# A drain of GpSimd in mid-run and another order of the first loads, in a kernel of a DFT, a channel mix and routed experts

## The chip, the cores and the metric

One core of one Trainium2 chip runs one program. The metric is device time in microseconds (us), first to last instruction of the core with the little that lies around it. In the text PE is the matmul engine (TensorE), DVE is VectorE, ACT is ScalarE, POOL is GpSimd and SP is SyncE, which here only issues DMAs. A "q" behind a name (SPq, POOLq) marks what an engine's sequencer does: issue, wait, branch, drain.

## The reference

```
X = fft(fft(x, axis=1), axis=2).real                  # x: 4 x 3072 x 256
xk, xr = mixes of X and X shifted by one position (mu_k, mu_r)
r = sigmoid(xr @ w_r);  y = r * (relu(xk @ w_k)**2 @ w_v)      # 256 -> 1024 -> 256
e = argmax(y @ w_gate);  g = softmax prob of e * sigmoid(y @ w_output_gate)[e]
out[token] = g * (relu(y @ w1[e]) @ w2[e])            # 8 experts, 12288 tokens
```

Four weights arrive as 64-bit floats and are turned into pairs of 32-bit parts (high and low) on the chip.

## The kernel before

Tile (the framework) orders the instructions of each engine by their priority, which follows the order in which the program text creates them, and by what they wait for. Each engine then runs its list in order.

**The first stage (lines 262 to 384).** `load_first_x` (L262) issues the load of the DFT constants and seven loads of `x` for batch 0 on SP's queue, and after them four loads of weights (`convert_r`, then three `convert_k`, L259 and L157). `a_steps` (L274) makes the first DFT pass: 13 PE products (L288) from the seven `xs` tiles, each copied back from PSUM by ACT (L102), and each finished `xs` tile is written to a scratch tensor `scr` in DRAM (L298, L301): from POOL's queue for batch 0, from ACT's queue for batches 1 to 3. When all seven writes have landed, `load` (L307) reads `scr` back transposed, as `raw` tiles (L312). DVE adds and subtracts halves of `raw` (`s`, `t`, `f`), PE makes the second pass (`ps`, L364) with the tables `tb`, then the passes over the channels, and the result is `xt`. `mix_steps` (L396) makes the inputs `rh`, `rl`, `kh`, `kl` of the first of 24 blocks (`b_block`, L498).

**Weight conversion.** `convert` (L202) issues a load into a `both` tile and notes it; `convert_rest` (L220) converts the oldest one: ACT takes the absolute value (`g`, L225), DVE shifts and masks the halves (`a`, `b`, `w`, five operations), ACT rounds to the high part `h`, and DVE makes the low part with two subtractions and additions. There are nine such units, one of `w_r`, four of `w_k`, four of `w_v`. At the top level (L554 to L572) the text stands in this order: first loads, `setup_first`, `setup_second` (the constant `mc`), the 13 products, two conversions, the first group of the second pass, the fifth weight load, a third conversion, and so on.

**The middle.** 24 blocks (512 positions each) run on PE with DVE and ACT; POOL writes each block's token numbers into expert lists (`lists`, 96 indirect DMAs, L491).

**The last stage.** `make_plan` (L721) makes on DVE a table `plan` of which expert each tile of 256 tokens belongs to. `extra` (L893, through the helper of L890) loads one number of it into a register of each engine. `pipeline` (L809) then runs 25 full tiles and five half tiles (numbers 55 to 59): it gathers tokens (L621, 55 indirect DMAs by POOL), multiplies by the expert's weights and stores with POOL (`out<-o`, L707, 55 indirect DMAs, one for each half tile, of which the stores of 55 to 59 are the last five). Behind it stands a conditional block (L895, `tc.If(extra > 0)`) for token counts that don't fit, which is skipped with this data. At the end of the program (L926) each engine drains and all of them meet.

The lines that matter most:

```
267        for i, (pool, tag, bufs) in enumerate(places):
269            load_x(first_x[i], 0, i)
270        for unit in early_units[:4]:
271            unit()
298   (POOL if b == 0 else ACT).dma_start(sv[:, :, 2 * w - 2:2 * w + 2], e...)
707   i = POOL.indirect_dma_start(out[:, :], bass.IndirectOffsetOnAxis(ap=ix[:, u, 1:2], axis=0),
893   extra = value(NTILE, NTILE + E, ...)
894   pipeline(list(range(-EARLY, MORE[0])) + list(range(NTILE, NTILE + HALVES)), EARLY)
895   with tc.If(extra > 0):
```

Of the kernel before, what the change touches and what calls it, by code (L numbers as in the profile page):

```python
# [26 lines left out]
EARLY = 3  # L27
MORE = [22, 26, 31, 38, NTILE]
HALVES = 5
CAP = NT + TT  # L30
ROW = 265
FAR = 1 << 20
# [63 lines left out]
def moe_kernel(ctx: ExitStack, tc: tile.TileContext, x, mu_k, mu_r, wk2, wv2, wr2, wg, wo, w1, w2,  # L96
# [4 lines left out]
    def act_copy(o, i, scale=1.0):  # L101
        return ACT.activation(out=o, in_=i, func=ACTF.Copy, scale=scale)  # L102
# [49 lines left out]
    def follow(i, earlier, kind, reason):  # L152
        for k in earlier:
            tc.add_manual_dep(i.ins, k.ins.name, mybir.DependencyInfo(kind, mybir.DependencyReason.DATA), reason=reason)

    def load_later(o, i):
        follow(SP.dma_start(o, i), raws[1:2], mybir.DependencyClass.NoSync, "the first groups come first")  # L157

    def split(h, l, src, eng=None):
        return act_copy(h, src), tt(l, src, h.bitcast(F32), ALU.subtract, eng)  # L160
# [23 lines left out]
    def setup_second():  # L184
        mc = bp.tile([128, 2, 2, 128], F32, name="mc", tag="y", bufs=1)
        SP.dma_start(mc, c_m.rearrange("p (a b c) -> p a b c", a=2, b=2))
        split(mh, ml, mc)
# [29 lines left out]
        load_later(both.rearrange("p (a b) -> p a b", a=src.shape[1]), src.bitcast(I32))  # L217
        loaded_w.append((h, l, both, a, b, g))

    def convert_rest():  # L220
        h, l, both, a, b, g = loaded_w.pop(0)
        lo, hi = both[:, 0:1024:2], both[:, 1:1024:2]
        w = bp.tile([128, 512], F32, name="cw", tag="mx")
        af, bf = a.bitcast(F32), b.bitcast(F32)
        ACT.activation(out=g, in_=hi.bitcast(F32), func=ACTF.Abs)  # L225
        DVE.tensor_scalar(a, hi, 3, 0x3FFFFFF8, ALU.logical_shift_left, ALU.bitwise_and)
        stt(a, hi, -0x40000000, a, ALU.bitwise_and, ALU.bitwise_or)
        stt(af, g, SMALLEST, af, ALU.is_ge, ALU.mult)
        DVE.tensor_scalar(b, a, -0x800000, None, ALU.bitwise_and)
        stt(w, lo.bitcast(U32), 2.0 ** -52, bf, ALU.mult, ALU.mult)  # L230
        flat = lambda t: t.rearrange("p a b -> p (a b)")
        act_copy(flat(h), af)
        tt(af, af, flat(h).bitcast(F32), ALU.subtract)
        tt(flat(l), af, w, ALU.add)

# [27 lines left out]
    def load_first_x():  # L263
        places = [(a1, "xs", 3)] * 3 + [(bp, "yh", 1), (bp, "yl", 1), (bp, "rs", 1), (bp, "row", 2)]
        SP.dma_start(fc, c_f)
        for i, (pool, tag, bufs) in enumerate(places):
            first_x.append(pool.tile([120, 2, 512], F32, tag=tag, name="xs", bufs=bufs))
            load_x(first_x[i], 0, i)
        for unit in early_units[:4]:
            unit()  # L270

    def a_steps(b):
        scr = dram.tile([24, 130, 256], F32, name="scr", tag="scr", bufs=2)
        sv = scr.rearrange("s (g m) d -> s g m d", g=5)  # L274
        for w in range(13):
            if w % 2 == 0:
                if b == 0:
                    e = xs = first_x[w // 2]
                else:
                    xs = a1.tile([120, 2, 512], F32, tag="xs", name="xs", bufs=3)  # L280
                    i = load_x(xs, b, w // 2)
                    follow(i, raws[2:3], mybir.DependencyClass.NoSync, "the first groups come first")
                    e = a1.tile([120, 2, 512], F32, tag="e", name="e", bufs=2)
            k_ = 120 if w < 12 else 96
            fs = slice(0, 120) if w < 12 else slice(120, 216)
            ps = pm.tile([120, 512], F32, tag="m", name="ps1")
            if b == 0:
                PE.matmul(ps[0:k_], fc[0:k_, fs], xs[0:k_, w % 2], start=True, stop=True)  # L288
                yield
            else:  # L290
                h = a1.tile([120, 512], F32R, tag="xh", name="xh")
                l = a1.tile([120, 512], F32R, tag="xl", name="xl")
                split(h[0:k_], l[0:k_], xs[0:k_, w % 2])
                yield
                mm3(ps[0:k_], fh[0:k_, fs], fl[0:k_, fs], h[0:k_], l[0:k_])
            act_copy(e[0:k_, w % 2], ps[0:k_])
            if w % 2:
                (POOL if b == 0 else ACT).dma_start(sv[:, :, 2 * w - 2:2 * w + 2], e.rearrange("p w d -> p (w d)"))  # L298
                yield
            elif w == 12:  # L300
                (POOL if b == 0 else ACT).dma_start(sv[:, 0:4, 24:26], e[0:96, 0])  # L301
            yield
        loaded = {}

# [248 lines left out]

    load_first_x()  # L554
    setup_first()
    setup_second()
    advance(0, 32)
    convert_rest()
    convert_rest()
    advance(0, 1)  # L560
    early_units[4]()
    convert_rest()
    advance(0, 4)
    setup_third()
    convert_rest()
    advance(0, 5)
    for _ in mix_steps(BLOCKS[0]):
        pass
# [5 lines left out]

    c1 = {}
    weights, xtile, meta, index, chunks, regs = {}, {}, {}, {}, {}, {}
    hq, outs, stores = {}, {}, []

    def open_c1():
        sa.close()  # L580
# [17 lines left out]
    def width(t):  # L598
        return 2 if t < NTILE else 1
# [88 lines left out]
    def m2(t, p):  # L688
        if p == 0:
            outs[t] = [pm.tile([128, D], F32, tag="m", name=f"o{u}") for u in range(width(t))]  # L690
        h, l = hq.pop((t, p))
        for u in range(width(t)):
            for a in range(2):
                f = 2 * p + a
                wh, wl = weights[t][2 + f // 4]
                cols = slice((f % 4) * D, (f % 4) * D + D)
                tok = slice(u * 128, u * 128 + 128)
                ps = outs[t][u]
                PE.matmul(ps, h[:, a, tok], wh[:, cols], start=f == 0, stop=False)  # L699
                PE.matmul(ps, l[:, a, tok], wh[:, cols], start=False, stop=False)  # L700
                PE.matmul(ps, h[:, a, tok], wl[:, cols], start=False, stop=f == 7)  # L701
        if p == 3:
            sc, ix = meta.pop(t), index.pop(t)
            o = bp.tile([128, 2, D], F32, tag="t1", name="o", bufs=2)
            for u in range(width(t)):
                ACT.activation(out=o[:, u], in_=outs[t][u], func=ACTF.Copy, scale=sc[:, u])
                i = POOL.indirect_dma_start(out[:, :], bass.IndirectOffsetOnAxis(ap=ix[:, u, 1:2], axis=0),  # L707
                                            o[:, u], None, bounds_check=NT - 1, oob_is_err=False)
                for k in stores[-4:]:
                    tc.declare_no_dep(i.ins, k.ins, reason="every token is in one list once: rows are distinct")  # L710
                stores.append(i)
            outs.pop(t)
            weights.pop(t)

# [171 lines left out]
    for _ in tail:  # L886
        pass
    sb.close()
    make_plan()
    value = lambda i, top, why: nc.values_load(  # L890
        c1["plan"][0:1, i:i + 1, 3:4].rearrange("p a b -> p (a b)"), min_val=0, max_val=top,
        skip_runtime_bounds_check_because=why)
    extra = value(NTILE, NTILE + E, "what is left of sums that add up to at most NTILE and E")  # L893
    pipeline(list(range(-EARLY, MORE[0])) + list(range(NTILE, NTILE + HALVES)), EARLY)
    with tc.If(extra > 0):  # L895
        total = value(0, NTILE, "a sum of rounded counts that add up to at most NT")
        halves = value(NTILE + 1, E, "at most one half tile of each expert")
# [32 lines left out]
```

## Time and profile before

| what | value |
|---|---|
| median of 3 runs | 1190.78 us (1190.38 to 1191.68) |
| the profiled execution's own time | 1189.58 us |
| its span, first to last instruction | 1187.8 us |
| busy: PE, DVE, ACT, POOL | 96%, 75%, 65%, 19% of the span |
| mean granted PE clock | 0.985 of full speed |
| DMAs issued by POOL | 96 + 55 + 55 indirect, 7 plain |

Busy time is what the profiler records of an engine's instructions; a PE that is busy is not a PE at its peak. The chain is the sequence of work that ended last, followed back from the end. Idle time of an engine counts only where that engine stands in the chain.

### The profile page before, as it was taken

What the parts mean: (1) busy time and instruction counts of PE and PEld (TensorE: products, weight loads), DVE (VectorE), ACT (ScalarE), POOL (GpSimd) and SP (SyncE); (2) the same over time, 40 slices, a digit from 0 to 9 for tenths busy, and PEclk for the clock granted to TensorE, in tenths of its full rate; (3) what the DMA queues carried; (4) which work ended last, traced back from release to release, by engine and by line L of the source; (5) the groups of instructions that cost most, each with busy time, mean ns of one, the idle gap of its engine ahead of it and who ended that gap; (6) DMA issues with size and microseconds to landing.
All of it is one profiled execution on the core that took longest, in us unless ns stands there. A gap on an engine that the chain in (4) does not pass through costs nothing.

```text
span 1187.8 us, 19728 instructions
## 1 busy us (share of the span) xinstructions
PE 1135.6 (96%) x6743; PEld 971.6 (82%) x6743; DVE 892.6 (75%) x2032; ACT 775.3 (65%) x1611; POOL 228.4 (19%) x228
## 2 busy tenths in 40 slices
PE   5499999999999999999999999999999999999994
PEld 1477888888888888888887888877999999999994
DVE  1899898578869768768857877776677777777782
ACT  3577777567777667767756666855376676667671
POOL 1000111111100111111111111123342433343220
PEclk9699999999999999999999999999999999999998
DMA  8753551214432215324100000202234133441580
GB/s 275 235 183 126 157 160 55 88 57 130 128 126 81 81 54 144 76 65 128 48 28 29 28 28 19 90 20 55 88 119 147 47 113 109 118 124 38 156 246 13
DMA packets 63176, 119.17 MB, mean 100 GB/s; under 512 B 14299, under 2 KB 41181, under 8 KB 62297
## 3 DMA queue, kind: packets, MB, share of 16 engines
q1 hardware_dynamic: 51015, 91.62, 25.2%
q0 software_dynamic: 9296, 16.76, 4.6%
q10 hardware_dynamic: 2754, 9.44, 2.8%
q8 instruction: 55, 0.90, 0.4%
q14 instruction: 56, 0.46, 0.2%
HBM read 116.43 MB, written 46.57 MB: 137 GB/s over the span
## 4 chain that ended last, share of the span: by engine, by line
PE 87%; DMA 3%; DVE 3%; issue 3%; ACT 1%; SPq 1%; POOL 0%; POOLq 0%; ACTq 0%
PE v L252 8%; PE v L253 7%; PE v L254 7%; PE psk L252 7%; PE psk L253 7%; PE psk L254 7%; PE hps L254 4%; PE hps L253 4%; PE hps L252 4%; PE o L701 4%; PE o L700 4%; PE o L699 4%; PE ps L364 4%; PE ps L252 2%; PE psr L252 2%
## 5 line engine op out<-in xcount | busy, mean ns | idle before, releaser
L491 POOL DMA_INDIRECT lists<-cid,pi x96 | 100.9, 1051 | 683.9 <-DVE pi L488 622.3
L108 DVE SCALAR_TENSOR_TENSOR t<-psk,t 128x512 f32<-128x512 f32 x192 | 132.3, 689 | 62.5 <-ACT t L530 60.3
L530 ACT ACTIVATE t<-psk 128x512 f32<-128x512 f32 x192 | 114.3, 597 | 97.6 <-PE psk L254 84.8
L105 DVE TENSOR_TENSOR ql<-t,qh 128x512 fp32r<-128x512 f32 x192 | 132.4, 690 | 37.0 <-ACT qh L102 35.2
L252 PE MATMUL psk<-kh,wkh 128*128 128x512 f32 x384 | 156.6, 408 | 2.2 <-DVE t L108 1.2
L252 PE MATMUL v<-qh,wvh 128*128 128x512 f32 x384 | 153.7, 400 | 0.2 <-ACT qh L102 0.2
L253 PE MATMUL v<-qh,wvl 128*128 128x512 f32 x384 | 152.0, 396 | 0.0
L253 PE MATMUL psk<-kh,wkl 128*128 128x512 f32 x384 | 151.6, 395 | 0.0
L254 PE MATMUL psk<-kl,wkh 128*128 128x512 f32 x384 | 151.1, 394 | 0.0
L254 PE MATMUL v<-ql,wvh 128*128 128x512 f32 x384 | 150.2, 395 | 0.0
L102 ACT ACTIVATE qh<-t 128x512 fp32r<-128x512 f32 x192 | 120.7, 629 | 42.3 <-DVE t L108 35.4
L684 ACT ACTIVATE hh<-hps 128x512 fp32r<-128x512 f32 (+1 forms) x120 | 67.4, 562 | 107.6 <-PE hps L254 89.9
L108 DVE SCALAR_TENSOR_TENSOR hl<-hps,hh 128x512 fp32r<-128x512 f32 (+1 forms) x120 | 77.5, 646 | 73.7 <-ACT hh L684 63.1
L621 POOL DMA_INDIRECT xg<-rows,ix x55 | 61.5, 1119 | 183.0 <-PE hps L254 48.1
L252 PEld LDWEIGHTS psk<-kh,wkh 128*128 128x128 f32 x384 | 72.5, 189 | 17.6 <-DVE t L108 1.6
L254 PEld LDWEIGHTS v<-ql,wvh 128*128 128x128 f32 x384 | 72.3, 188 | 17.2 <-DVE ql L105 0.4
L254 PEld LDWEIGHTS psk<-kl,wkh 128*128 128x128 f32 x384 | 72.3, 188 | 16.7
L252 PEld LDWEIGHTS v<-qh,wvh 128*128 128x128 f32 x384 | 72.3, 188 | 15.3 <-ACT qh L102 0.9
L253 PEld LDWEIGHTS psk<-kh,wkl 128*128 128x128 f32 x384 | 72.6, 189 | 14.2
L253 PEld LDWEIGHTS v<-qh,wvl 128*128 128x128 f32 x384 | 72.5, 189 | 14.3
L108 DVE SCALAR_TENSOR_TENSOR mx<-xt,omu,mx 128x512 f32<-128x512 f32 x96 | 71.9, 749 | 6.3 <-ACT mx L402 5.3
L105 DVE TENSOR_TENSOR wlb<-raw,whb 128x512 fp32r<-128x512 f32 x112 | 73.3, 686 | 2.5 <-ACT whb L102 0.8
(219 smaller groups left out, 3102.5 us busy)
## 6 DMA issues: line engine op xcount, KB each, us to landing
raw<-in_moe_w SPq DMA_DIRECT2D x112, 512.0 KB
rows<-row SPq DMA_DIRECT2D x24, 530.0 KB
raw<-scr SPq DMA_DIRECT2D x24, 512.0 KB
out<-zeros SPq DMA_DIRECT2D x48, 256.0 KB
xs<-in_x SPq DMA_DIRECT2D x24, 480.0 KB
scr<-e ACTq DMA_DIRECT2D x18, 480.0 KB
tb<-in_c_t SPq DMA_DIRECT2D x20, 256.0 KB
scr<-xs POOLq DMA_DIRECT2D x6, 480.0 KB
```

The source lines that it names most:

```text
L102: return ACT.activation(out=o, in_=i, func=ACTF.Copy, scale=scale)
L105: return (eng or DVE).tensor_tensor(out=o, in0=a, in1=b, op=op)
L108: return DVE.scalar_tensor_tensor(out=o, in0=a, scalar=s, in1=b, op0=op0, op1=op1, **kw)
L252: PE.matmul(ps, ah, bh, start=start, stop=False)
L253: PE.matmul(ps, al, bh, start=False, stop=False)
L254: return PE.matmul(ps, ah, bl, start=False, stop=stop)
L364: PE.matmul(ps[:, a * 128:a * 128 + 128], f[:, a, c, par * 128:par * 128 + 128], tb[:, a, c], start=c == 0, stop=c == 1)
L491: i = POOL.indirect_dma_start(lists[:, :], bass.IndirectOffsetOnAxis(ap=pi[:, u:u + 1], axis=0), cid[:, n, u], None, bounds_check=E * CAP ...
L530: ACT.activation(out=t, in_=ps, func=ACTF.Relu)
L621: POOL.indirect_dma_start(xg[:, u], None, rows[0:nr], bass.IndirectOffsetOnAxis(ap=ix[:, u, 0:1], axis=0), bounds_check=nr - 1, oob_is_err ...
L684: marks[:] = [last, ACT.activation(out=h, in_=ps, func=ACTF.Relu), stt(l, ps, 0.0, h.bitcast(F32), ALU.max, ALU.subtract)]
L699: PE.matmul(ps, h[:, a, tok], wh[:, cols], start=f == 0, stop=False)
```

## The change

- **Drain.** After the store of half tile 57 (`DRAIN_AT = NTILE + HALVES - 3`), POOL gets a drain instruction. It is ordered behind that store and ahead of the stores of 58 and 59, on POOL alone.
- **Count.** The load of `extra` into registers is created after `pipeline` instead of before it.
- **Loads dealt.** The loads of `w_r` and of two parts of `w_k` are issued after the second, third and fourth load of `x`, not after the seventh; the fourth weight load comes after the 13 products in the text, as does `setup_second`.
- **Conversions.** The first three run on DVE alone (the absolute value as a mask, the rounding as a copy) and are created before the 13 products; the fourth is created after the first group.
- **Scratch writes.** Those of batch 0 are issued on ACT's queue, as those of the other batches are.

```diff
+DRAIN_AT = NTILE + HALVES - 3
...
-    def convert_rest():
+    def convert_rest(alone=False):
...
-        ACT.activation(out=g, in_=hi.bitcast(F32), func=ACTF.Abs)
+        if alone:
+            DVE.tensor_scalar(g.bitcast(I32), hi, 0x7FFFFFFF, None, ALU.bitwise_and)
+        else:
+            ACT.activation(out=g, in_=hi.bitcast(F32), func=ACTF.Abs)
...
-        act_copy(flat(h), af)
+        DVE.tensor_copy(flat(h), af) if alone else act_copy(flat(h), af)
...
             load_x(first_x[i], 0, i)
-        for unit in early_units[:4]:
-            unit()
+            if 1 <= i <= 3:
+                early_units[i - 1]()
...
-                (POOL if b == 0 else ACT).dma_start(sv[:, :, 2 * w - 2:2 * w + 2], e.rearrange("p w d -> p (w d)"))
+                ACT.dma_start(sv[:, :, 2 * w - 2:2 * w + 2], e.rearrange("p w d -> p (w d)"))
...
     setup_first()
+    for _ in range(3):
+        convert_rest(True)
+    advance(0, 32)
+    early_units[3]()
     setup_second()
-    advance(0, 32)
-    convert_rest()
-    convert_rest()
     advance(0, 1)
     early_units[4]()
+    advance(0, 4)
     convert_rest()
-    advance(0, 4)
     setup_third()
-    convert_rest()
     advance(0, 5)
...
                 stores.append(i)
+                if drains and t > DRAIN_AT:
+                    follow(i, drains[:1], mybir.DependencyClass.NoSync, "what is written from here on is retired at the end")
+            if t == DRAIN_AT:
+                drains.append(POOL.drain())
+                follow(drains[0], stores[-width(t):], mybir.DependencyClass.NoSync, "this much is retired first")
...
+    pipeline(list(range(-EARLY, MORE[0])) + list(range(NTILE, NTILE + HALVES)), EARLY)
     value = lambda i, top, why: nc.values_load(
...
     extra = value(NTILE, NTILE + E, "what is left of sums that add up to at most NTILE and E")
-    pipeline(list(range(-EARLY, MORE[0])) + list(range(NTILE, NTILE + HALVES)), EARLY)
     with tc.If(extra > 0):
```

## Rows read from the trace of the kernel before

**Rows 1.** Windows of the first stages: span, busy by engine, clock, DMA share, GB/s

```profile
25.90:46.40 20.50, 7.57 (x27) 5.97 (x28) 18.46 (x42) 9.79 (x28) 2.21 (x4) 0.50 0.72 237
46.40:60.00 13.60, 9.04 (x47) 7.48 (x47) 11.63 (x27) 9.94 (x26) 0.00 (x0) 0.88 0.84 257
60.00:80.00 20.00, 17.74 (x89) 14.05 (x88) 19.36 (x38) 14.02 (x32) 0.00 (x0) 1.00 0.61 194
120.00:140.00 20.00, 20.00 (x101) 16.05 (x100) 17.17 (x36) 15.22 (x36) 4.37 (x4) 1.00 0.42 123
```

**Rows 2.** Chain of what ended last, first 40 us: start, us, what

```profile
8.29 19.09 DMA both<-in_moe_w_k
...
30.37 4.86 DMA scr<-xs
35.38 3.86 DMA raw<-scr
39.26 0.69 DVE s L105
```

**Rows 3.** ACT in order of time: start, us, instruction, idle time before it

```profile
25.07 0.68 ACT L225 ACTIVATE cg<-both 128x512 f32<-128x512 f32 x1 [7.26 <-DMA both<-in_moe_w_r]
...
27.40 0.68 ACT L225 ACTIVATE cg<-both 128x512 f32<-128x512 f32 x1 [0.69 <-DMA both<-in_moe_w_k]
...
28.98 1.07 ACT L102 ACTIVATE xs<-ps 120x512 f32<-120x512 f32 x2
```

**Rows 4.** POOL's first write, and DMA queues with packets from 11.19 to 16.4 us

```profile
11.19 0.77 POOL L298 DMA_DIRECT2D scr<-xs  x1 [8.45 <-ACT xs L102]
...
q1 hardware_dynamic: 338, 1.26, 104.6%
```

**Rows 5.** DVE in order of time, before and after the first raw tile

```profile
25.07 0.43 DVE L226 TENSOR_SCALAR ca<-both 128x512 int32<-128x512 int32 x1 [21.53 <-DMA both<-in_moe_w_r]
...
42.20 0.68 DVE L105 TENSOR_TENSOR wkl<-ca,cw 128x512 fp32r<-128x512 f32 x1
...
48.38 0.69 DVE L105 TENSOR_TENSOR wkl<-ca,cw 128x512 fp32r<-128x512 f32 x1
```

**Rows 6.** Group of DVE's mask operations, first 100 us: busy, mean ns, idle

```profile
L226 DVE TENSOR_SCALAR ca<-both 128x512 int32<-128x512 int32 x5 | 2.1, 425 | 21.9 <-DMA both<-in_moe_w_r 21.5 <-DMA both<-in_moe_w_k 0.4
```

**Rows 7.** POOL's last three stores in order of time

```profile
1158.09 0.98 POOL L707 DMA_INDIRECT out<-o,ix  x1 [7.44 <-ACT o L706]
1166.48 0.98 POOL L707 DMA_INDIRECT out<-o,ix  x1 [7.42 <-ACT o L706]
1171.97 0.98 POOL L707 DMA_INDIRECT out<-o,ix  x1 [4.51 <-ACT o L706]
```

**Rows 8.** Sequencers at the end: ns min/median/max, first and last start in us

```profile
L890 SPq TENSOR_LOAD <-plan x1: 273/273/273, 1155.4 to 1155.4; - x1
...
L890 POOLq TENSOR_LOAD <-plan x1: 498/498/498, 1171.7 to 1171.7; - x1
...
L895 POOLq EVENT_SEMAPHORE  x5: 17/42/43, 1175.2 to 1175.7; - x5
...
L895 POOLq INC_SWDGE_SEM  x1: 2335/2335/2335, 1175.8 to 1175.8; - x1
...
L926 SPq EVENT_SEMAPHORE  x14: 17/28/28, 1178.1 to 1187.7; - x14
...
L926 POOLq DRAIN  x3: 44/107/8812, 1178.2 to 1187.5; - x3
L926 SPq DRAIN  x3: 7/7/13, 1178.8 to 1187.2; - x3
```

**Rows 9.** POOL's sequencer at the program's start, same columns

```profile
L914 POOLq INC_SWDGE_SEM  x1: 27/27/27, 0.1 to 0.1; - x1
...
L914 POOLq DRAIN  x1: 188/188/188, 0.3 to 0.3; - x1
```

**Rows 10.** ACT's issues of scratch writes, batches 1 to 3, same columns

```profile
L298 ACTq DMA_DIRECT2D scr<-e x18: 322/323/873, 76.7 to 536.2; - x18
```

More of the change, by code (lines that the diff above doesn't have):

```diff
@@ L154, in follow, with load_later @@
             tc.add_manual_dep(i.ins, k.ins.name, mybir.DependencyInfo(kind, mybir.DependencyReason.DATA), reason=reason)
-    def load_later(o, i):
-        follow(SP.dma_start(o, i), raws[1:2], mybir.DependencyClass.NoSync, "the first groups come first")
+    def load_later(o, i, eng=None):
+        follow((eng or SP).dma_start(o, i), raws[1:2], mybir.DependencyClass.NoSync, "the first groups come first")
     def split(h, l, src, eng=None):
@@ L297, in a_steps @@
             if w % 2:
-                (POOL if b == 0 else ACT).dma_start(sv[:, :, 2 * w - 2:2 * w + 2], e.rearrange("p w d -> p (w d)"))
+                ACT.dma_start(sv[:, :, 2 * w - 2:2 * w + 2], e.rearrange("p w d -> p (w d)"))
                 yield
             elif w == 12:
-                (POOL if b == 0 else ACT).dma_start(sv[:, 0:4, 24:26], e[0:96, 0])
+                ACT.dma_start(sv[:, 0:4, 24:26], e[0:96, 0])
             yield
@@ L576, in moe_kernel @@
     weights, xtile, meta, index, chunks, regs = {}, {}, {}, {}, {}, {}
-    hq, outs, stores = {}, {}, []
+    hq, outs, stores, drains = {}, {}, [], []
     def open_c1():
```

## The prediction

> **What bounds the kernel now.** I read the windows first, then the chain of waits from the start, then ACT, DVE and POOL in order of time, and last what the sequencers do behind the last store. From about 100 us on the matmul engine is never idle (20.00 of 20.00 us in the window from 120 us [rows 1]), and nothing in the change touches its work there. So the change can only pay at the two ends, and a shift at the start comes through to the end undiminished, since everything behind it is bound by PE and is queued behind it.
>
> *The start.* The chain runs through a weight load, then the scratch write, the raw load and DVE [rows 2]. The reader is to see why a weight load stands there: ACT runs in order, and its absolute value for the first conversion waits 7.26 us, until 25.07, for `w_r`, with the PSUM copies of `xs` queued behind it; the next one holds it to 27.40 [rows 3]. The last copies start at 28.98, the last write is on its way at 30.37 and lands 4.86 us later, and the first raw tile reaches DVE at 39.26 [rows 2, 3]. DVE meanwhile waits 21.53 us until 25.07 [rows 5], then is the busiest engine: 18.46 of 20.50, 11.63 of 13.60 and 19.36 of 20.00 us [rows 1].
>
> *The end.* POOL's last store starts at 1171.97 [rows 7]. Behind it stand its register load, a branch, a few semaphore waits at 1175.2 to 1175.7, INC_SWDGE_SEM of 2.34 us from 1175.8, and a drain of 8.81 us from 1178.2 that ends at 1187.0 [rows 8]. SP's last drain ahead of the meeting is done at 1178.9 [rows 8]; all others wait for POOL.
>
> **The change part by part.**
>
> *Drain.* At the program's start, with no DMA behind it, POOL's drain takes 0.19 us [rows 9]; at the end it takes 8.81, and the two that follow it at once take 0.107 and 0.044 [rows 8]. Between the first and the long one lie 213 DMAs issued by POOL (96, 55 and 55 indirect ones and 7 plain ones by the table of the profile). So I read its time as a charge for each DMA since the last drain: 8.81 / 213 = 0.041 us. After the change two stores lie behind the drain in mid-run: 0.19 + 2 x 0.04 = 0.27 us instead of 8.81. What is late next is SP, whose drain is done 0.7 us after POOL's begins. So the end gains 1187.0 - 1178.9 = **8.1 us**. The bounds: 0 if the last drain is as long as now; 8.1 + 2.3 = 10.4 if INC_SWDGE_SEM, 0.03 us at the start [rows 9], shrinks with it, since SP's waits begin only when it ends, at 1178.1 [rows 8]. I keep 8.1, because only the drain is known to be short right behind another.
>
> The drain in mid-run has 204 of these DMAs ahead of it (seven have gone to ACT, two stores come later), 204 x 0.041 = 8.4 us. It can start when store 57 is issued, 1158.09 + 0.98 = 1159.1, and ends at 1167.5. Queued behind it on POOL are two stores alone (the last gather is past). Store 58, ready at 1166.48, goes 1.0 us late, and nobody waits for it but the end; store 59, ready at 1171.97, finds POOL free since 1168.5 [rows 7]. So the price is nothing; it starts only when the drain takes more than 1171.97 - 0.98 - 0.30 - 1159.07 = 11.6 us, and from there each us costs one. If it also waits for store 57 to land, which for the last store is at most 3.7 us (from 1171.97 until the semaphore waits are over at 1175.7 [rows 7, 8]), 8.4 + 3.7 = 12.1 costs 0.5.
>
> The Trainium skill, VectorE: DVE Perf Modes, section The DRAIN you can't avoid, says that the drains of a program's pre- and postamble are about 12 ns, the same on all five engines. SP's 7 to 13 ns agree, POOL's 8812 ns does not [rows 8]. By that rule the drain would be worth nothing, which is rival C below; the row decides against it.
>
> *Count.* The register loads of `extra` already stand last on their engines: on SP at 1155.4, on POOL at 1171.7, after the issue of the last store [rows 8]. Creating them later in the text moves nothing: 0, with at most the load's own 0.5 us either way.
>
> *Loads dealt.* SP issues the same loads in another order. Each of the three weight loads put ahead of `x` pushes the later `x` loads by its own time, which is the distance at which two of them landed: 27.40 - 25.07 = 2.33 us [rows 3]. The last `x` had landed before the first weights, so at 25.07 - 2.33 = 22.7 at the latest; now it lands at 29.7 at most (22.7 + 7.0). At best it lands where the loads aren't delayed at all, at 22.7. I take 27.5: the bytes up to there are the same as before, and the writes begin sooner (below). That each `x` load is also issued one to three issues later costs nothing, as SP is far ahead of the transfers. `mc` and the fourth weight load keep their place behind the others, and what needs them stands behind the raw tiles.
>
> *Conversions.* One unit alone on DVE is three mask operations of 0.43, five of 0.69 as the one at 42.20 [rows 5, 6], and a copy between these two durations: 5.2 to 5.5 us; three are 16 us. They lie in DVE's idle 21.53 us [rows 5], as their loads land one by one, the first as third of SP's queue some 10 us sooner than now; the third is done about 5 us after its load. ACT loses 3 x 1.3 us of work and, above all, the two waits. If that cover is gone (loads as late as now), DVE is done at 35, no later than today.
>
> *Scratch writes on ACT.* ACT's issue of such a write takes 0.32 us [rows 10], seven are 2.3 us on an engine that is mostly idle there. POOL's first write, issued at 11.19, had moved no packet by 16.4: only SP's queue shows any [rows 4]. The Trainium skill, DMA: Bandwidth & Descriptors, section Issuing engines are not separate DMA queues, says that another issuing engine saves only the time of initiating. By that the move would be worth (0.77 - 0.32) us for a write, hidden; the five microseconds without a packet say more.
>
> *Sum of the start.* After the last `x` at 27.5 come a product and copies (2 us as I estimate from the 1.4 us between the last copies and the write under way), then the write: bounded by 0.8 us (192 KB at the 257 GB/s of rows 1) and the 4.86 of today; I take 3.5, since fewer writes are in flight at once. The raw load then goes at 33.0 instead of 35.38: **2.4 us** (from 5.5 earlier to 2 later by the bounds). And DVE is freer: today six operations of the fourth and the end of the third conversion stand among the first folds, from 42.20 to 48.38, 3.5 us in all [rows 5]. Now the third is done by then and the fourth falls mostly into the wait for raw: I take **2.6 us** of 0 to 3.5. Since DVE is what PE waits for up to 100 us, both count in full: 5.0 us, with bounds of -2 and 9.
>
> Sum against the profiled execution: 1189.58 - 8.1 - 5.0 = 1176.5; the median of the runs lies 1.2 above that execution, so **1177.7**.
>
> **The rivals.**
>
> B, *the start gains nothing.* ACT now issues DMAs, in order; if its first writes must wait for loads to land, as ACT waited for weights in rows 3, the copies of `xs` stand behind them and the last write goes no sooner. For it: the last `x` does land later. Against: no conversion is in ACT's way. The end alone: 1190.8 - 8.1 = 1182.7.
>
> C, *the change doesn't do what it says at the end*: the last drain is long whatever lies between, a fixed price after any POOL DMA. For it: one execution shows one long drain. Against: 0.107 us for the next. 1190.8 - 5.0 = 1185.8.
>
> D, *INC_SWDGE_SEM shrinks too*: 1177.7 - 2.3 = 1175.4.
>
> E, *slower: PE's clock stays low.* The granted clock is 0.50 (1.2 GHz) from 25.9 to 46.4 us, a stretch in which PE works 7.57 of 20.50 us; it rose some 7 us after the first raw tile reached DVE [rows 1, 2]. With `x` spaced out PE pauses more often. If it stayed at 1.2 GHz until 80 us, some 7 of the 9.04 us and all of the 17.74 us [rows 1] would double, 25 us, less PE's idle 6.8 us in those windows: 18 us, so 1195.9. It decides from 13.1 + 6.8 = 20 us of PE work at the low level. Against: from 60 us on the level is 1.00 although PE still pauses [rows 1].
>
> F, *neither end gains*: 1190.8.
>
> **How the numbers follow.** My forecast 0.50, B 0.22, C 0.12, D 0.06, E 0.05, F 0.05. Beside the forecast stands its own range, 1173.5 to 1181, from the bounds of the start. The range for all is 1173.0 to 1186.5: it takes in B, C and D and leaves out E, F and their edges. No change that can be told is within 0.2%, 2.4 us. Faster: all but E and F, 0.90; same 0.05; slower 0.05.
>
> **What would show it.** Drain: POOL's drain in mid-run of 8 us or so between stores 57 and 58, the last drain under 0.5 us, and SP's as the last of the others. Start: no idle ACT before 25 us on a weight load; DVE busy between 12 and 28 us; the first raw load issued near 33. Conversions: no `wkl` between the first folds. Count: register loads where they were. Wrong would be: a last drain of 8 us; a raw load at 35 or later; an ACT that stands before its scratch writes; a clock of 0.5 beyond 60 us.

## The result, and the profile after

The changed kernel takes 1176.42 us (median of 6 runs, 1173.89 to 1179.4) against 1190.73: a ratio of 0.9877, 95% interval 0.9859 to 0.9895, some 14 us faster. The forecast was 1177.7. The profiled execution took 1178.56 us, with a span of 1176.8; it is one of the longer ones of the six; what the record says of that is told below.

*The end.* POOL's last five stores in order of time (start, us, instruction, idle time before it):

```profile
1144.34 1.01 POOL L711 DMA_INDIRECT out<-o,ix  x1 [0.31 <-ACT whb L103]
1148.81 0.98 POOL L711 DMA_INDIRECT out<-o,ix  x1 [3.46 <-ACT o L710]
1157.23 0.98 POOL L711 DMA_INDIRECT out<-o,ix  x1 [7.44 <-ACT o L710]
1167.15 0.97 POOL L711 DMA_INDIRECT out<-o,ix  x1 [8.94 <-ACT hh L688]
1171.16 0.97 POOL L711 DMA_INDIRECT out<-o,ix  x1 [3.03 <-ACT o L710]
```

The sequencers of the same stretch (ns min/median/max, first and last start). A drain is an instruction of the sequencer; in these traces nothing behind it on its engine starts before it ends (here store 58 at 1167.15, the drain until 1166.3). INC_SWDGE_SEM is another, at the end of the skipped block:

```profile
L719 POOLq DRAIN  x1: 9287/9287/9287, 1157.0 to 1157.0; - x1
```

```profile
L900 POOLq TENSOR_LOAD <-plan x1: 505/505/505, 1170.9 to 1170.9; - x1
```

```profile
L904 POOLq INC_SWDGE_SEM  x1: 235/235/235, 1175.0 to 1175.0; - x1
```

```profile
L935 POOLq DRAIN  x3: 46/107/217, 1175.2 to 1176.5; - x3
L935 SPq DRAIN  x3: 7/7/13, 1175.9 to 1176.2; - x3
```

The drain in mid-run lies between stores 57 and 58, and only store 58 is late, which nobody waits for. Behind the last store the drain takes 0.22 us instead of 8.81 and INC_SWDGE_SEM 0.24 instead of 2.34 [rows 8]. From the last store's start to the end of the span it is 1176.8 - 1171.16 = 5.6 us; before it was 1187.8 - 1171.97 = 15.8 [rows 7]. The end gained 10.2 us. The register load of the count still starts with the last store on POOL (1170.9 us, the store 1171.16; before 1171.7 and 1171.97).

*The start.* First the chain, then the windows that answer to [rows 1] (span, busy by engine, clock, DMA share, GB/s), then three instructions of DVE: the first of the conversions, the last of the third and the last of the fourth:

```profile
3.11 7.42 DMA both<-in_moe_w_r
...
10.54 14.72 DMA xs<-in_x
...
29.36 4.39 DMA scr<-xs
...
33.87 3.76 DMA raw<-scr
...
37.65 0.69 DVE s L106
```

```profile
25.90:46.40 20.50, 9.95 (x45) 7.79 (x44) 13.62 (x36) 8.60 (x29) 0.53 (x1) 0.74 0.73 247
46.40:60.00 13.60, 10.91 (x47) 8.12 (x45) 12.44 (x24) 10.70 (x26) 0.00 (x0) 0.77 0.82 256
60.00:80.00 20.00, 18.16 (x87) 14.18 (x86) 16.08 (x33) 11.94 (x25) 0.00 (x0) 0.99 0.74 209
```

```profile
10.55 0.43 DVE L227 TENSOR_SCALAR cg<-both 128x512 int32<-128x512 int32 x1 [6.91 <-DMA both<-in_moe_w_r]
...
27.47 0.69 DVE L106 TENSOR_TENSOR wkl<-ca,cw 128x512 fp32r<-128x512 f32 x1
...
34.04 0.69 DVE L106 TENSOR_TENSOR wkl<-ca,cw 128x512 fp32r<-128x512 f32 x1
```

DVE now converts from 10.55 us on, not from 25.07 [rows 5], and is done with the three that it makes alone at 28.2 us and with the fourth at 34.7, before the first fold (the additions of halves of `raw`, from 37.65 us). Up to the raw load no weight that ACT waits for stands in the chain any more; at its head stands `w_r`, for which a load of `x` waits, as the last section shows. But the first raw load goes at 33.87, against 35.38 [rows 2]: 1.5 us. Behind it DVE is still the fullest engine from 80 to 100 us (19.68 of 20 us, against 19.67 before), but no longer from 60 to 80 us: 16.08 us against 19.36 [rows 1].

*The middle*, in which nothing was changed. The first count product (kps) of block 1 and that of block 24, of the kernel before and after (line, ns, start):

```profile
L479 PE MATMUL kps<-oh,ones_tri x1: 190/190/190, 121.6 to 121.6; 128*128 128x32 bf16 x1
L479 PE MATMUL kps<-oh,ones_tri x1: 191/191/191, 838.1 to 838.1; 128*128 128x32 bf16 x1
```

```profile
L483 PE MATMUL kps<-oh,ones_tri x1: 190/190/190, 120.4 to 120.4; 128*128 128x32 bf16 x1
L483 PE MATMUL kps<-oh,ones_tri x1: 189/189/189, 832.6 to 832.6; 128*128 128x32 bf16 x1
```

At block 1 the changed kernel is 1.2 us ahead, at block 24 it is 5.5: the blocks between take 712.2 us instead of 716.5, by some 0.2 us each. At the last store the lead is down to 0.8 us: from block 24 to the last store this execution took 338.6 us. In twelve others (that of before, and those of the experiments but the one whose last store is held back) the same stretch takes 333.9 to 334.9 us with the old start, in three, and 334.4 to 337.4 with the changed one, in nine. A part of the loss is the clock. The same window of the changed kernel and of the kernel before:

```profile
840.00:850.00 10.00, 9.28 (x65) 9.29 (x66) 4.60 (x21) 2.75 (x5) 2.18 (x3) 0.83 0.21 56
840.00:850.00 10.00, 8.28 (x71) 8.08 (x70) 8.31 (x48) 4.13 (x7) 3.91 (x4) 1.00 0.01 1
```

A clock of 0.83 instead of 1.00 over 10 us costs at most 1.7 us of the 4.7, and four of the nine have such a row too (0.83 to 0.85). The rest is open, and so is whether the changed start brings some of it. PE is not full there in the kernel before either.

### The profile page after: what moved, and what is told of

Its sections match the earlier page's. It is cut to its first block, busy times and chain, and to the rows that moved or that the text cites. A ratio compares the mean times of both kernels' runs of the same rounds, so it can differ in the third digit from the quotient of the medians.

```text
span 1176.8 us, 19714 instructions
## 1 busy us (share of the span) xinstructions
PE 1136.5 (97%) x6743; PEld 973.6 (83%) x6743; DVE 894.6 (76%) x2038; ACT 772.4 (66%) x1605; POOL 224.6 (19%) x221
## 4 chain that ended last, share of the span: by engine, by line
PE 89%; DMA 4%; issue 3%; DVE 2%; ACT 1%; POOL 0%; SPq 0%; POOLq 0%; ACTq 0%
PE v L256 8%; PE v L258 7%; PE v L257 7%; PE psk L256 7%; PE psk L258 7%; PE psk L257 7%; PE hps L258 4%; PE hps L256 4%; PE hps L257 4%; PE o L705 4%; PE o L704 4%; PE o L703 4%; PE ps L368 4%; PE ps L256 2%; PE psr L257 2%
## 5 line engine op out<-in xcount | busy, mean ns | idle before, releaser
L258 PEld LDWEIGHTS v<-ql,wvh 128*128 128x128 f32 x384 | 72.1, 188 | 18.2 <-DVE ql L106 1.5
L256 PE MATMUL hps<-xh,wha 128*128 128x256 f32 (+1 forms) x256 | 73.2, 286 | 2.8 <-issue 2.6
```

The lines of the kernel that those rows point to most:

```text
L256: PE.matmul(ps, ah, bh, start=start, stop=False)
L258: return PE.matmul(ps, ah, bl, start=False, stop=stop)
```

## The experiments

All ratios are to the kernel before, run beside it on the same chip, with 95% intervals. "The end" is the time from the start of POOL's last store to the end of the span, "the blocks" that from the count product of block 1 to that of block 24.

### The drain alone, and all but the drain

Two kernels: the kernel before with the drain added (its first stage as before), and the changed kernel with these lines taken out:

```
-                if drains and t > DRAIN_AT:
-                    follow(i, drains[:1], ...)
-            if t == DRAIN_AT:
-                drains.append(POOL.drain())
-                follow(drains[0], stores[-width(t):], ...)
```

> The kernel before with the drain in mid-run alone (between stores 57 and 58); loads, conversions, scratch writes and count as before. Theory (the end and the start add up; the end gives what the profile of the changed kernel shows behind its last store): POOL's drain in mid-run takes 9 us hidden, the last one 0.2 us instead of 8.8, and INC_SWDGE_SEM 0.24 us instead of 2.3; 10.2 us faster, 1180.5, ratio 0.9914. Rival 1 (only the drain belongs to it, the short INC_SWDGE_SEM comes from the other order of the start): 8.1 us, 1182.6, ratio 0.993. Rival 2 (the last drain was short because of the start, for instance because POOL no longer writes the scratch): no change, 1190.7, ratio 1.000.

> The changed kernel without the drain: all of the start and the late count. Theory: the end costs as before (last drain 8.8 us, INC_SWDGE_SEM 2.3 us), so that it is 10.2 us slower than the changed kernel, 1186.6, ratio to before 0.9965; the start is worth 4.1 us on the median, 0.8 to 5 by the execution. Rival 1 (the start gives nothing at the last store, the executions of the changed kernel that are faster owe it to something else): 1190, ratio 0.999. Rival 2 (start as forecast, 5 us): 1185.7, ratio 0.9958.

Measured: 1179.93 us with the drain alone, 0.9915 (0.9901 to 0.993); 1184.5 without it, 0.995 (0.9934 to 0.9965). The ends are 5.2 and 15.2 us. POOL's drains at the end, of the drain alone and then of the kernel without it:

```profile
L932 POOLq DRAIN  x3: 46/107/223, 1176.9 to 1178.2; - x3
```

```profile
L929 POOLq DRAIN  x3: 40/107/8232, 1173.7 to 1182.5; - x3
```

The drain is worth 10 us by itself, the short INC_SWDGE_SEM comes with it (0.24 us with the drain alone, 2.2 without), and all the rest is worth 6 us (4.2 to 7.9). Together that is 16 us, against 14.3 measured for the whole change (12.5 to 16.8): the two parts add up within the intervals. The second kernel's first rival, a start that gives nothing, falls.

### What a drain's length goes by

The changed kernel with its drain at full tile 10, and with its drain one store later:

```
-DRAIN_AT = NTILE + HALVES - 3
+DRAIN_AT = 10                      # first kernel
+DRAIN_AT = NTILE + HALVES - 2      # second kernel
```

> The changed kernel with its drain behind the stores of full tile 10 instead of half tile 57, so that 27 stores and about 21 gathers of POOL lie behind it. Theory (a charge for each DMA of POOL since the last drain, 0.041 us): last drain 0.2 + 48 x 0.041 = 2.2 us, the drain in mid-run shorter than 9.3 by the same, about 7.3 us; 2 us slower than the changed kernel, 1178.4, ratio 0.9897. Rival 1 (a fixed price of the first drain after any DMA of POOL, paid whenever some have been issued since): last drain again 8.8 us, 1186. Rival 2 (any drain before the end makes the last one short, whatever lies between): last drain 0.2 us, 1176.4.

> The changed kernel with its drain one store later, between the last two stores (58 and 59). Theory (the price is what sticks out past the readiness of the last store): the drain starts when store 58 is issued, near 1166.7 us of the profiled execution, takes 9.3 us, and the last store starts at 1176.3 instead of 1171.2: 5.1 us slower than the changed kernel, 1181.5, ratio to before 0.9923. Rival (the drain waits also for the landing of store 58, up to 3.7 us): 8.8 us slower, 1185.2, ratio 0.9954. Second rival (it lets the next store pass or costs nothing): 1176.4.

Measured: 1179.22 us, 0.9906 (0.989 to 0.9923), and 1181.12 us, 0.9928 (0.991 to 0.9946). At tile 10 the last drain is neither 0.2 nor 8.8 nor 2.2 us:

```profile
L935 POOLq DRAIN  x3: 46/107/3811, 1172.0 to 1176.4; - x3
```

So it does grow with what lies behind the last drain, but by 3.81 / 46 = 0.083 us for each DMA, twice the charge that I had worked out. With the drain between stores 58 and 59 the last store has to wait (the last two stores of that kernel):

```profile
1162.90 0.97 POOL L711 DMA_INDIRECT out<-o,ix  x1 [7.43 <-ACT o L710]
1172.93 0.97 POOL L711 DMA_INDIRECT out<-o,ix  x1 [9.05 <-issue]
```

Undisturbed the last store comes 5.5 us behind store 58 (1167.16 after 1161.64 in the kernel with its drain at tile 10), here 10.0: 4.5 us stick out. The median is 4.7 us above the changed kernel's; by the ratios it is 6, with some 3 us of uncertainty. The drain doesn't wait for the store to land: it ends 8.2 us after the store's issue, which its count accounts for (below).

The next kernel settles the count; it also moves all tiles by 64 bytes, which is told further below.

```
+    const.tile([128, 16], F32, name="pad")
...
+        if n == 19:
+            follow(POOL.drain(), done, ..., "the lists alone")
```

> Two separate things in one run, on the changed kernel. First, 64 unused bytes per partition ahead of the working tiles: kh, kl, qh and ql then leave 32 over when divided by 128, as in the kernel before, though their order and distances from each other are those of the changed kernel. Theory (the remainder decides): the 24 blocks take 716.5 us as before, 4.2 us slower, 1180.6. Rival (the order of the tiles, or the distances between them, decide): 712.3 us, 1176.4. Second, one more drain of POOL behind the list writes of the twentieth of 24 blocks: ahead of it lie 80 list writes and nothing else of POOL's DMAs. Theory (each DMA of POOL costs the same 0.041 us at the next drain): about 3.3 us, and the drain at half tile 57 some 3.3 us shorter than 9.3. Rival (the list writes, of 8 bytes for each of 128 rows, cost a drain next to nothing; the gathers and stores, of 1 KB rows, cost 0.075 us each): under 0.5 us beyond the wait for the last write to land, and 9.3 us again at 57.

Its two drains in mid-run, and the issues that stand just ahead of their ends:

```profile
L506 POOLq DRAIN  x1: 10647/10647/10647, 731.6 to 731.6; - x1
```

```profile
734.68 0.97 POOL L496 DMA_INDIRECT lists<-cid,pi  x1 [0.30 <-issue]
```

```profile
L722 POOLq DRAIN  x1: 3572/3572/3572, 1153.0 to 1153.0; - x1
```

```profile
1153.21 0.97 POOL L714 DMA_INDIRECT out<-o,ix  x1 [7.43 <-ACT o L713]
```

A drain's row begins while DMAs ahead of it are still being issued, so what counts is the time from the end of the last issue to the drain's end: 731.6 + 10.65 - 735.65 = 6.6 us for 80 list writes, 0.083 us each. The list writes cost as much as gathers and stores; the rival falls. All drains, read in this way (the other kernels repeat 2, 204, 211 and 213 within 0.02 us):

| POOL's DMAs since the last drain | drain, us | of the kernel |
|---|---|---|
| 1 | 0.14 | drain between 58 and 59, at the end |
| 2 | 0.22 | changed, at the end |
| 46 | 3.81 | drain at tile 10, at the end |
| 80 | 6.6 | lists alone |
| 124 | 2.4 | lists alone, at store 57 |
| 160 | 4.5 | drain at tile 10, in mid-run |
| 204 | 8.1 | changed, in mid-run |
| 205 | 8.2 | drain between 58 and 59, in mid-run |
| 206 | 8.23 | without the drain |
| 211 | 8.7 | drain alone, in mid-run |
| 213 | 8.81 | before |

Up to 80 it is 0.083 us for each. From 160 to 213 it is 0.083 us for each above 107. So some hundred of the oldest are already done with by then, without a drain and without a visible price (in the kernel with 124 it must be 96 of them). Bytes don't count: the seven plain writes, six of them of 480 KB, make 0.6 us between 204 and 211, 0.083 each as the list writes do. Whether the charge goes by the DMA or by its rows is not shown; each list write, gather and store has up to 128. The Trainium skill, SBUF — State Buffer, section SBUF size: 192, 224, or 256, says that 16 KiB of each partition are set aside for a ring of descriptors of the DMAs that GpSimd generates. No run here shows that ring; that a limited store takes its oldest entries back when it is full would fit the table, and is not shown.

### Where the tiles lie

The changed kernel creates the tiles of the first conversions between those of `x`, and the framework places tiles in SBUF in the order of their first creation. So kh, kl, qh and ql, which stream through PE in the blocks, begin at 45408, 20832, 29024 and 35168 bytes instead of 66208, 41632, 49824 and 55968; the weights stay where they were. Two kernels part this from everything else. The first is the kernel before with the same instructions in the same order on every engine, and the places of the changed one; the second is the changed kernel with the places of the one before:

```
+            if 1 <= i <= 3:
+                made.append(first_tiles(i - 1))   # first kernel: created early, loaded as before
...
-            load_x(first_x[i], 0, i)              # second: all x tiles created, then loaded
+        for i in range(7):
+            load_x(first_x[i], 0, i)
```

> The kernel before with every instruction and its order as before, and only the places of its tiles in SBUF (the on-chip memory) as in the changed kernel: the tiles of the first conversions are allocated between those of x, not after them. In the profiles so far the 24 blocks, from the first count product (kps) of block 1 to that of block 24, take 716.5 and 717.0 us with the start of before and 712.2 to 712.7 us with the changed start, though PE runs the same products in nearly the same order. Theory (the places of the operands decide it): 712.3 us here, the whole 4.2 us faster, 1185.7 against 1189.9, ratio 0.9965. Rival 1 (what decides is the small shift in the order of instructions that the changed start leaves on PE, DVE and ACT): 716.5 us, ratio 1.000. Rival 2 (places and order by half each): 714.5, ratio 0.998.

> The changed kernel with every instruction and its order as it is, and only the places of its tiles in SBUF as in the kernel before (all tiles of x are allocated ahead of those of the conversions). Theory (places decide the length of the 24 blocks): first to last count product 716.5 us instead of 712.3, 4.2 us slower than the changed kernel, 1180.6, ratio to before 0.992; what is left of the start's gain is that at block 1, 1 to 1.5 us, beside the 10 us of the end. Rival 1 (the order decides): 712.3 us, 1176.4, ratio 0.988. Rival 2 (half each): 1178.5.

Measured: 1187.26 us, 0.9973 (0.9962 to 0.9983), and 1181.22 us, 0.9915 (0.9898 to 0.9932). The count products of blocks 1 and 24, of the first and then of the second:

```profile
L487 PE MATMUL kps<-oh,ones_tri x1: 190/190/190, 122.0 to 122.0; 128*128 128x32 bf16 x1
...
L487 PE MATMUL kps<-oh,ones_tri x1: 190/190/190, 834.3 to 834.3; 128*128 128x32 bf16 x1
```

```profile
L484 PE MATMUL kps<-oh,ones_tri x1: 189/189/189, 119.8 to 119.8; 128*128 128x32 bf16 x1
...
L484 PE MATMUL kps<-oh,ones_tri x1: 189/189/189, 836.2 to 836.2; 128*128 128x32 bf16 x1
```

712.3 and 716.4 us: the places alone make the blocks 4.2 us shorter, both ways; by its ratio the first kernel as a whole gains 3.2 us (2.0 to 4.5). It is in the products. Two groups from 160 to 780 us, before and after (busy us, mean ns of one):

```profile
L253 PE MATMUL v<-qh,wvl 128*128 128x512 f32 x309 | 122.4, 396 | 0.0
L253 PE MATMUL psk<-kh,wkl 128*128 128x512 f32 x309 | 121.9, 395 | 0.0
```

```profile
L257 PE MATMUL v<-qh,wvl 128*128 128x512 f32 x311 | 122.3, 393 | 0.0
L257 PE MATMUL psk<-kh,wkl 128*128 128x512 f32 x312 | 122.2, 392 | 0.0
```

What of the places decides was tried by three more kernels: the 64 bytes above, 32 bytes (with the earlier `w_v` loads of the next section), and a third order of the tiles.

```
+    const.tile([128, 8], F32, name="pad")            # 32 bytes
...
+        a = bp.tile(..., tag="qh", bufs=3)           # third order: qh, ql, yh, rs,
+        b = bp.tile(..., tag="ql", bufs=3)           #   kl, yl, t1, row, kh
+        early_x = {3: x_tile(3), 5: x_tile(5)}
+        both = bp.tile(..., tag="kl")
```

> The kernel with the earlier loads of w_v, and 32 unused bytes per partition ahead of all working tiles in SBUF. In the changed kernel the tiles kh, kl, qh and ql that stream through PE begin at a byte address that leaves 96 over when divided by 128, in the kernel before 32; here it is 0. Theory (the remainder decides how long one product takes: 0.2325 us from one to the next for most with 32, 0.2275 to 0.23 with 96; at 0 there is at most as much as at 96): first to last count product 712 us or less; if 0 is better than 96 by as much as 96 is than 32, 708, and 1170.7 in all. Rival 1 (only the order of the tiles, which of them are neighbours, counts): 712.3 us, 1174.9 as without the pad. Rival 2 (96 was the best place): 716.5 us, 1179.

> The changed kernel, every instruction and its order kept, with a third arrangement of its tiles in SBUF: kh and kl (which stream through PE for psk) about where the kernel before has them (66208 and 41312 instead of 45408 and 20832), qh and ql (which stream for v) lower than in the changed kernel (20832 and 26976). In the profiles so far the time from one product to the next, between 160 and 780 us, is 232.4 ns for psk<-kh,wkl and 232.7 for v<-qh,wvl in the kernel before, 229.3 and 229.5 in the changed one. Theory (a product's pace goes with the place of the tile that streams in it): v stays at 229.5, psk goes back to 232.4; the 24 blocks take about 714.4 us, 2 us more than the changed kernel. Rival 1 (the arrangement as a whole decides, for instance which tiles ACT, DVE and the DMAs touch near the ones that PE reads): both at 232.5, 716.5 us, or both at 229.4, 712.3 us. Rival 2 (the smaller address is the better one): v below 229.0.

The mean time from one product's start to the next's, in ns (worked out from the trace between 160 and 780 us, steps under 0.28 us), and the blocks in us:

| kernel | psk<-kh,wkl | v<-qh,wvl | psk<-kh,wkh | blocks |
|---|---|---|---|---|
| before | 232.4 | 232.7 | 232.3 | 716.5 |
| places back | 232.5 | 232.8 | 232.3 | 716.4 |
| changed | 229.3 | 229.5 | 231.3 | 712.2 |
| places only | 228.9 | 229.0 | 231.5 | 712.2 |
| 32 bytes on | 229.4 | 229.5 | 229.7 | 711.9 |
| 64 bytes on | 228.3 | 229.5 | 230.8 | 711.2 |
| third order | 232.9 | 230.2 | 230.7 | 713.6 |

Over the six kinds of `psk` and `v` products the changed kernel is 2.0 ns faster in the mean, 4.5 us for the 96 products of each of 23 blocks, so the products account for the whole. The clock is not it: it is 1.00 from 160 to 780 us in all seven kernels. The remainder by 128 is not it: 64 bytes on it is that of the kernel before, and the blocks stay short. In the third order psk<-kh,wkl falls back to its old pace with kh at its old place, while v keeps most of its gain; but psk<-kh,wkh stays fast. So a product's pace partly goes with the place of the tile that streams in it, as the theory had it, and partly with the arrangement. By what mechanism is open. The Trainium skill, SBUF — State Buffer, section Terms, says that PE and ACT have ports of their own to this memory and that DMAs use others; by that no other engine and no DMA would stand in PE's way at its port. No run here shows the ports, and the section says nothing of what a tile's place costs.

The kernel with 32 bytes took 1173.76 us, 0.9861 (0.9846 to 0.9876), that with 64 bytes 1175.39, 0.987 (0.9855 to 0.9885), the third order 1176.36, 0.9897 (0.988 to 0.9914).

### The parts of the start

Scratch writes back on POOL, the first two `w_v` loads earlier, and the weights behind all `x` loads again (the conversions stay on DVE alone, the places are kept):

```
-                ACT.dma_start(sv[...], ...)                        # first kernel
+                (POOL if b == 0 else ACT).dma_start(sv[...], ...)
...
     convert_rest()                                                 # second
+    convert_v(0)
+    convert_v(1)
     setup_third()
...
-            if 1 <= i <= 3:                                        # third
-                early_units[i - 1]()
+        for unit in early_units[:3]:
+            unit()
```

> The changed kernel with the scratch writes of batch 0 back on POOL's queue; all else as changed. Theory (what the move gave is the time between the last copy of xs and the landing of the last write: 0.8 us of waiting for POOL to issue it and 0.5 us of a longer transfer): the first raw load is issued near 35.2 us instead of 33.9, block 1 begins 1.3 us later, 1177.7. Rival 1 (the writes on POOL move no packet until 16 us and pile up behind it): raw load at 37 or later, 1180. Rival 2 (the move gave nothing, the writes wait for the loads of x in either case): raw load at 33.9, 1176.4.

> The changed kernel with the loads of the first two quarters of w_v put ahead of setup_third and of the zeroing of the lists in the text, so that they are issued near 41 us instead of 45.1 and 45.5. Theory (in the changed kernel ACT, and DVE behind it, stands from 46 to 53.5 us on these loads, which took the place of the wait for the first weights, and gives back what the start won): the wait ends 4 us sooner, block 1 begins 2 to 4 us sooner, 1173.4, ratio 0.986. Rival 1 (the transfers are the bound there, mean DMA share 0.8 between 20 and 60 us; the raw loads come later by as much): no change, 1176.4. Rival 2 (the second raw load is delayed by them and PE waits for it): 2 us slower, 1178.4.

> The changed kernel with the three weight loads issued behind all seven loads of x, as in the kernel before, and with the places of its tiles kept; the conversions stay on VectorE alone and ahead of the first products in the text. Theory (the dealing trades the two: x lands sooner without it, the weights later, and DVE converts until about 41 us instead of 34, in front of the first folds): first raw load issued 3 us sooner, near 31, the first fold no sooner than 38 to 41, block 1 begins within 1 us of the changed kernel, 1176.4. Rival 1 (x bounds the start, the conversions fit in beside it): block 1 3 us sooner, 1173.4. Rival 2 (the conversions come in the way of the folds): block 1 3 us later, 1179.4.

| kernel | first raw load | block 1 | median | ratio |
|---|---|---|---|---|
| writes on POOL | 34.87 | 119.7 | 1177.01 | 0.9889 (0.9868 to 0.9909) |
| `w_v` earlier | 34.38 | 119.3 | 1174.87 | 0.9855 (0.9835 to 0.9875) |
| weights behind `x` | 33.40 | 124.7 | 1182.89 | 0.9934 (0.9921 to 0.9948) |

The first two can't be told from the changed kernel: with the writes on POOL the first raw load is 1.0 us later than in the changed kernel's profile, but within the range of that start (33.87 to 36.36, below), and block 1 is no later; the Trainium skill, DMA: Bandwidth & Descriptors, section Issuing engines are not separate DMA queues, has it so, that another issuing engine saves no more than the time of initiating, and here the trace agrees. The premise of the second was misread: the chain shows a `w_v` load of 7.90 us at 45.54, but ACT's own idle time ahead of it was 0.96 us, and the next one's 2.23; the rest of the transfer lay beside other work. It moved only the first two of four `w_v` loads; for the third ACT still waits 3.41 us in that kernel.

The third is 6.5 us slower than the changed kernel, and its block 1 begins 4.3 us later: its second rival, at more than the 3 us that I had put on it, though the raw load goes 0.5 us sooner. DVE's conversions stand in front of the folds:

```profile
23.10 0.43 DVE L233 TENSOR_SCALAR cg<-both 128x512 int32<-128x512 int32 x1 [19.45 <-DMA both<-in_moe_w_r]
...
38.49 0.69 DVE L109 SCALAR_TENSOR_TENSOR ca<-cg,ca 128x512 f32<-128x512 f32 x1
39.10 0.69 DVE L106 TENSOR_TENSOR s<-raw 128x512 f32<-128x512 f32 x1
```

And the raw load isn't 3 us sooner, because ACT stands 5.18 us until a weight has landed, with a scratch write and two copies of `xs` behind it:

```profile
25.63 0.32 ACTq L310 DMA_DIRECT2D scr<-xs  x1
26.00 1.08 ACT L103 ACTIVATE xs<-ps 120x512 f32<-120x512 f32 x2 [5.18 <-DMA both<-in_moe_w_k]
```

## Why the prediction was right

- **Drain: right in mechanism, its size too small by 2.1 us.** I took 8.1 and named 10.4 as the bound for the case that INC_SWDGE_SEM shrinks too; the end gained 10.2. I gave that case 0.06 as a rival of its own; it belongs to the drain, since both go by the same number of DMAs (INC_SWDGE_SEM: 0.24 us for 2, 1.11 for 46, 2.2 for 206).
- **The charge of 0.041 us: wrong.** Dividing 8.81 by all 213 DMAs assumed that all still count. It is 0.083 for each of some 106. For the drain in mid-run both give 8 us (8.4 foretold, 8.1 measured), which is why the plan held; for a drain placed early, 2.2 against 3.8.
- **Price in mid-run: nothing, right.** Half a tile later it sticks out, as the rule of 11.6 us has it, and it doesn't wait for the store to land.
- **Count: nothing, right** as far as the row shows, which is where it was; it was not run by itself.
- **Start: its number came near by luck (5.0 us foretold, 6 measured without the drain), its working was wrong.** I had 2.4 us for the raw load and 2.6 for DVE among the folds, both to come through in full. In the five profiles with the whole changed start (the changed kernel, without the drain, drain at tile 10, at 58, places back) the raw load goes at 33.87 to 36.36, 34.9 in the mean, against 35.3 in three with the old start (before, drain alone, places only); block 1 begins at 119.8 to 121.3, 120.4 in the mean, against 122.0. So the start gives 1.6 us, 0.4 of it at the raw load. The step that failed is "both count in full", with its premise that DVE is what PE waits for up to 100 us. For a while the gain is there. The first product of `v`, in the kernel before and the changed one:

```profile
L252 PE MATMUL v<-qh,wvh x384: 390/394/500, 68.3 to 826.5; 128*128 128x512 f32 x192
L256 PE MATMUL v<-qh,wvh x384: 388/394/503, 64.5 to 820.9; 128*128 128x512 f32 x192
```

It starts at 63.3 to 64.7 us in the five profiles against 68.3 to 69.0 in the three, 4.6 us sooner in the mean; 3.0 of these are lost before the count product of block 1. In that stretch DVE has time to spare: from 60 to 80 us it is busy 16.1 to 16.9 of 20 us in the five, 18.2 to 19.4 in the three. What holds the work up there was not tested. One candidate is ACT, which in the changed kernel waits for the last two `w_v` loads, and in the kernel before does not:

```profile
67.89 0.68 ACT L229 ACTIVATE spare<-both 128x512 f32<-128x512 f32 x1 [2.23 <-DMA both<-in_moe_w_v]
...
78.60 0.68 ACT L229 ACTIVATE spare<-both 128x512 f32<-128x512 f32 x1 [0.92 <-DMA both<-in_moe_w_v]
```

- **What stands in its place: the places of the tiles**, 4.2 us over the 24 blocks, of which the prediction said that "nothing in the change touches its work there". 1.6 + 4.2 = 5.8, against 6 us measured without the drain.
- **The total: 13.1 us foretold, 14.3 measured, near by luck.** The end gave 2.1 us more than forecast, the start 3.4 less, and the places 4.2 that the forecast had not. That makes 16.0; the last 1.7 are within the interval, or lost in the last stage. There "a shift at the start comes through to the end undiminished" does not hold for this profile, whose lead goes from 5.5 us to 0.8 behind block 24.
- **Loads dealt: the direction was right** (the `x` land later, at 25.3 instead of 22.7 at the latest; I took 27.5), and without the dealing the conversions would have cost more than they gave.
- **Scratch writes: nothing, as the hidden 0.45 us have it.** That "the five microseconds without a packet say more" did not come true: with the writes back on POOL block 1 begins no later.
- **Rivals.** B (the start gives nothing) falls with the kernel without the drain, though its mechanism, ACT's writes waiting for a load, is seen in the kernel with the weights behind `x`. C falls with the last drain of 0.22 us. E falls: from 60 to 80 us the clock is 0.99. Before that it is 0.74 (0.50 in [rows 1]) with PE busy 9.95 us instead of 7.57, and then 0.77, lower than the 0.88 of [rows 1]. F falls with the ratio.

## What to carry to other kernels

In this program GpSimd's last drain grew with the DMAs that it had issued since the drain before (8.81 us behind 213, 0.22 behind 2), and the program's end waited for it. Where a profile shows such a drain, put one in mid-run where GpSimd has that time to spare (8 us here), as late as that allows, and look at how far behind it the next DMA is ready. Moving the first creation of a tile can change where all tiles lie, and with it the pace of a matmul-bound middle by half a per cent: compare the middle of two traces block by block before a gain or a loss is put down to the stage that was edited. And read a wait from the idle time of the engine, not from the length of a transfer in the chain.

## What the runs showed that I had not expected

- **A load can wait for another that has nothing to do with it.** With the loads dealt, SP issues its loads in one go only up to 6.7 us; then the last three `x` loads take 8.66 us to be issued (start, us from the first to the last, count):

```profile
5.96 0.52 SPq L158 DMA_DIRECT2D both<-in_moe_w_k  x1
6.70 8.66 SPq L263 DMA_DIRECT2D xs<-in_x  x3
```

With all `x` loads first, the seven go in one go:

```profile
1.29 6.06 SPq L269 DMA_DIRECT2D xs<-in_x  x7
```

The second of those three went at 10.54, when `w_r` had landed (DVE starts on it at 10.55), the third at 14.59. By the trace each of these issues waits on the completion semaphore that it uses itself and that an earlier load had used last, and ACT's wait of 5.18 us above is one on the semaphore of a weight load in the same way. My sentence that later issues cost nothing, "as SP is far ahead of the transfers", did not reckon with that.
- **The last stage varies**: 333.9 to 338.6 us from block 24 to the last store in thirteen profiles. The changed kernel's six runs spread over 5.5 us, those of the kernel before beside it over 3.1.
- **No version was shown to beat the changed kernel.** The one with earlier `w_v` loads and 32 bytes has the lowest median, but its interval overlaps the changed kernel's.
